# Loading q in 6 KB rows, with the layouts that follow from it, in a fused attention and token-mixing kernel

## The chip, the cores and the metric

The kernel runs on one core of one Trainium2 chip. The metric is device time in microseconds (us), the median over a kernel's executions. Each run is called fast or slow by its clock and by how far it lies above the fastest of its kernel. Matrix products are on TensorE (PE in the profile, PEld its weight loads), element-wise work on VectorE (DVE), exponentials on ScalarE (ACT), casts on GpSimd (POOL). Most DMAs are issued by SyncE (SP).

## The reference, cut to what matters

```python
# q [8, 16, 384, 64], k and v [8, 4, 384, 64]; float32
k, v   = np.repeat(k, 4, axis=1), np.repeat(v, 4, axis=1)
scores = np.matmul(q, k.transpose(0, 1, 3, 2)) / 8
attn   = softmax(scores)                       # over the keys
x      = np.matmul(attn, v).transpose(0, 2, 1, 3).reshape(8, 384, 1024)
wq, wk = x @ w_q, x @ w_k                      # [8, 384, 64]
W_tok  = np.einsum('bsd,btd->bst', wq, wk) / 8
mixed  = np.einsum('bst,btd->bsd', W_tok, x)
out    = np.maximum(mixed, 0.0) @ w_out        # [8, 384, 1024]
```

## The kernel before

A scheduler in the kernel's own code decides the order of instructions when the kernel is built, with estimates of each engine's clock. Eight batches overlap: while one batch is in attention, earlier ones are in the mixing part. These are the parts that the change and the argument touch.

```python
P, C, G, D = 128, 3, 4, 64    # partitions, groups of 128 tokens, heads per key head, head size

def ld(dst, src, a, z, c0=0, c1=C):   # token = 3 p + c: 768 B runs for each head
    nc.sync.dma_start(out=dst[:, a:z, c0:c1],
                      in_=src[b, a:z].rearrange("h (p c) d -> p h c d", p=P)[:, :, c0:c1])
...
# scores: two matmuls on the two row halves of the array
for u in range(2):
    nc.tensor.matmul(out=ps[:, u, :], lhsT=KT[lo:hi, kp * C + kc, :],
                     rhs=QT[lo:hi, t0:t0 + G, :].rearrange("k i p -> k (i p)"), ...)
...
# attend: after 12 matmuls, divide by the row sum ("the scaling"); 96 of these in the run
xnats[b] = x_p.tile([P, C, Hq, D], BF16, name="xnat", bufs=3)
nc.vector.reciprocal(out=rcp, in_=avv[:, :, D])
nc.vector.tensor_tensor(out=xnats[b][:, c, h0:h0 + G, :], in0=avv[:, :, :D],
                        in1=rcp.to_broadcast([P, G, D]), op=ALU.mult)
...
# output of 128 tokens: 512 KB, one 4 KB row for each partition
dst = out[b].rearrange("(p c) n -> c p n", c=C)[c]
nc.sync.dma_start(out=dst, in_=osb)
...
def after_s(b, s):                    # called after score group s of batch b
    n = b + 1
    if b == 0 or n >= B: return
    if s == 0:    load(n)
    elif s == 5:  cast(n); start_tr(n)
    elif s in (9, 11, 13, 15): tr_dma(n, (s - 9) // 2)
```

The softmax here doesn't subtract the row's maximum and nothing guards it: scores larger than these inputs give would overflow.

## Time and profile before

| | before |
|---|---|
| median of 3 runs (range) | 224.09 us (223.12 to 225.83) |
| profiled run: its time (slow state), its span | 226.12 us, 224.3 us |
| batch 2's first score starts | 45.45 us |
| from there to the end of the last matmul | 175.3 us |
| last output and end | 3.6 us |

The span is the sum of the last three rows, and I use these three terms.

This one profile of the kernel before is of a run that the record calls slow, and its clock shows it: 0.58 for 6.5 us from 45.5 us on, after TensorE had waited 2.9 us for q. The run `scaling_alone` below (one execution, its state unknown) begins with the same kernel. There TensorE waited 2.6 us at the same place and kept its full clock. The two lines are batch 2's first score, with the wait before it, and the stretch from 45.5 to 52 us (its columns are explained in the prediction; the 1.00 is the clock):

```profile
45.04 0.39 PE L259 MATMUL sc<-QT,KT 64*128 64x512 bf16 x2 [2.62 <-DMA QT<-qb]
...
45.50:52.00 6.50, 6.50 (x84) 3.53 (x83) 3.77 (x11) 5.38 (x6) 1.22 (x4) 1.00 1.02 267
```

In that execution the first two terms are 45.0 and 172.9. So some 2.4 us of the 175.3 above are not in every execution. Fast runs of the kernel before have a mean clock of 0.992 to 1.000, this one 0.985.

### The profile page before, as it was taken

The page shows a single profiled execution, that of the slowest core. Times are in us where ns is not written, and L with a number is a line of the kernel's source. Part 1 is how long each engine was busy: PE and PEld are TensorE (multiplying, and loading weights), DVE is VectorE, ACT ScalarE, POOL GpSimd, SP SyncE. Part 2 cuts the span into 40 slices and gives each one's busy share as a digit, 9 for nine tenths or more (in the row PEclk, how much of TensorE's full clock was granted, in tenths as well). Part 3 has the DMA queues.
Part 4 walks back from the last instruction along what each step waited for, and adds up shares of the span by engine and source line. Part 5 has one row for each costly group of instructions (what it writes and reads, how often), then busy time and mean ns, then how long its engine had stood idle before and what let it go on. Part 6 is the DMA issues. An engine that isn't in the chain of part 4 may idle for free.

```text
span 224.3 us, 5470 instructions
## 1 busy us (share of the span) xinstructions
PE 214.2 (95%) x2217; PEld 113.6 (51%) x2244; DVE 145.2 (65%) x365; ACT 140.6 (63%) x146; POOL 52.1 (23%) x97
## 2 busy tenths in 40 slices
PE   8999999589999999999999999999999999999993
PEld 5666665245545545454555546554555553434441
DVE  2355786834697758865887648874679569576332
ACT  3599998747788778887887887887888600000000
POOL 1385678406300540045016100620000000000000
PEclk9999999959999999999999999999999999999999
DMA  6996999999399979999999998989224422242424
GB/s 174 324 327 170 410 386 325 136 237 323 65 183 215 335 166 187 222 338 216 223 229 342 154 213 260 281 205 154 99 91 53 143 93 93 93 190 93 180 101 187
DMA packets 71688, 46.09 MB, mean 205 GB/s; under 512 B 42736, under 2 KB 67568, under 8 KB 71664
## 3 DMA queue, kind: packets, MB, share of 16 engines
q1 hardware_dynamic: 71520, 45.62, 77.6%
q8 instruction: 17, 0.28, 0.5%
q10 hardware_dynamic: 144, 0.13, 0.2%
q14 instruction: 7, 0.06, 0.1%
HBM read 23.59 MB, written 12.58 MB: 161 GB/s over the span
## 4 chain that ended last, share of the span: by engine, by line
PE 74%; DMA 14%; DVE 3%; SPq 3%; POOL 3%; issue 1%; DVEq 0%
PE bank L408 37%; PE bank L282 13%; PE sc L259 12%; DMA qraw<-in_q_dram 12%; PE bank L331 4%; SPq L129 3%; PE bank L384 3%; PE bank L362 2%; DMA QT<-qb 2%; PE bank L322 1%; POOL qb L158 1%; DVE osb L421 1%; PE bank L349 1%; DVE msb L389 1%; POOL wqk_sb L596 1%
## 5 line engine op out<-in xcount | busy, mean ns | idle before, releaser
L263 ACT ACTIVATE pt<-sc 128x1024 bf16<-128x1024 f32 x144 | 138.9, 1023 | 34.6 <-PE sc L259 34.4
L408 PE MATMUL bank<-wout_sb,msb 128*128 128x512 bf16 x357 | 91.7, 382 | 1.3 <-issue 0.5
L408 PEld LDWEIGHTS <-msb 128*128 128x128 bf16 x384 | 33.8, 98 | 42.4 <-issue 13.7
L259 PE MATMUL sc<-QT,KT 64*128 64x512 bf16 x288 | 47.5, 387 | 3.1 <-DMA QT<-qb 2.9
L282 PEld LDWEIGHTS <-pt 128*128 128x128 bf16 x1152 | 41.9, 98 | 15.8 <-issue 9.9
L282 PE MATMUL bank<-vext,pt 128*128 128x65 bf16 x1152 | 46.9, 195 | 0.4 <-DVE osb L421 0.2
L421 DVE COPY osb<-bank 128x512 f32<-128x512 f32 (+1 forms) x49 | 33.1, 677 | 21.7 <-PE bank L408 20.5
L289 DVE TENSOR_TENSOR xnat<-bank,rcp 128x256 bf16<-128x256 f32 x96 | 40.8, 425 | 3.3
L389 DVE TENSOR_SCALAR msb<-bank 128x384 bf16<-128x384 f32 x64 | 32.5, 551 | 9.5 <-PE bank L384 9.0
L287 DVE RECIPROCAL rcp<-bank 128x4 f32<-128x4 f32 x96 | 16.9, 176 | 17.6 <-PE bank L282 16.7
L158 POOL CAST qb<-qraw 128x768 bf16<-128x768 f32 x30 | 24.0, 827 | 17.4 <-DMA qraw<-in_q_dram 15.1
L153 POOL CAST kb<-kraw 128x192 bf16<-128x192 f32 x30 | 9.2, 347 | 67.3 <-DMA kraw<-in_k_dram 67.3
L259 PEld LDWEIGHTS <-KT 64*128 64x128 bf16 x288 | 12.4, 94 | 24.1 <-issue 17.2
L117 PE MATMUL bank<-idle 128*128 128x256 bf16 x80 | 14.8, 324 | 1.0 <-DVE idle L562 1.0
L331 PE MATMUL bank<-xT,wqk_sb 128*128 128x384 bf16 x64 | 11.7, 327 | 0.0
L117 PEld LDWEIGHTS <-idle 128*128 128x128 bf16 x80 | 7.9, 114 | 6.6 <-issue 4.0
L384 PE MATMUL bank<-wT,Csb 64*128 64x384 bf16 x32 | 10.6, 332 | 0.4 <-DVE rcp L287 0.3
L384 PE MATMUL bank<-wq,Csb 64*128 64x384 bf16 x32 | 10.6, 332 | 0.0
L599 POOL CAST wout_sb<-wld 128x1024 bf16<-128x1024 f32 x8 | 8.1, 1040 | 4.1 <-DMA wld<-in_moe_w_out_dram 4.1
L366 DVE CAST Csb<-bank 128x512 bf16<-128x512 f32 x8 | 5.5, 688 | 5.2 <-PE bank L362 5.2
L337 DVE CAST wT<-bank 128x384 bf16<-128x384 f32 x8 | 4.5, 558 | 6.7 <-PE bank L331 6.7
L323 DVE COPY xT<-bank 128x1024 bf16<-128x1024 bf16 x10 | 6.9, 688 | 2.5 <-PE bank L322 2.5
(33 smaller groups left out, 70.1 us busy)
## 6 DMA issues: line engine op xcount, KB each, us to landing
out_dram<-osb SPq DMA_DIRECT2D x23, 512.0 KB, 3.1
qraw<-in_q_dram SPq DMA_DIRECT2D x15, 768.0 KB, 7.4
wld<-in_moe_w_out_dram SPq DMA_DIRECT2D x4, 1024.0 KB, 9.5
kraw<-in_k_dram SPq DMA_DIRECT2D x7, 384.0 KB, 4.3
vraw<-in_v_dram SPq DMA_DIRECT2D x7, 384.0 KB, 8.9
qraw<-in_q_dram SPq DMA_DIRECT2D x1, 512.0 KB, 5.3
kraw<-in_k_dram SPq DMA_DIRECT2D x2, 192.0 KB, 3.7
vraw<-in_v_dram SPq DMA_DIRECT2D x2, 192.0 KB, 6.3
```

Source lines behind the costliest of these rows:

```text
L117: nc.tensor.matmul(out=bank_ps[i][:, :256], lhsT=idle[:, :P], rhs=idle, start=True, stop=True)
L158: eng.tensor_copy(out=nats[b][1][:, :, kp, :, u, :].rearrange("p c i d -> p i c d"), in_=raws[b][2][:, h0:h0 + G])
L259: nc.tensor.matmul(out=ps[:, u, :], lhsT=KT[lo:hi, kp * C + kc, :], rhs=QT[lo:hi, t0:t0 + G, :].rearrange("k i p -> k (i p)"), start=True, ...
L263: nc.scalar.activation(out=pt.rearrange("k u i p -> k u (i p)"), in_=ps, func=AF.Exp, scale=attn_scale)
L282: nc.tensor.matmul(out=ps[:, i * DE:i * DE + D + 1], lhsT=tiles[kc][:, u, i, :], rhs=vext[:, 2 * kp + u, kc, :D + 1], start=(kc == 0), sto ...
L287: nc.vector.reciprocal(out=rcp, in_=avv[:, :, D])
L289: nc.vector.tensor_tensor(out=xnats[b][:, c, h0:h0 + G, :], in0=avv[:, :, :D], in1=rcp.to_broadcast([P, G, D]), op=ALU.mult)
L331: nc.tensor.matmul(out=ps, lhsT=wqk_sb[:, dc, :], rhs=xT[:, dc].rearrange("d c p -> d (c p)"), start=(dc == 0), stop=(dc == DC - 1))
L384: nc.tensor.matmul(out=bank_ps[i][:, :S], lhsT=Csb[lo:hi, j * P:(j + 1) * P], rhs=w[lo:hi, :], start=True, stop=True)
L389: nc.vector.tensor_scalar_max(out=msb[:, dc, :], in0=bank_ps[i][:, :S], scalar1=0.0)
L408: nc.tensor.matmul(out=ps, lhsT=msbs[b][:, dc, c * P:(c + 1) * P], rhs=wout_sb[:, dc, half * NH:(half + 1) * NH], start=(nd == 0), stop=(n ...
L421: nc.vector.tensor_copy(out=osb[:, n0:n1], in_=ps[:, n0 - half * NH:n1 - half * NH])
```

## The change

Its intent is larger packets and an earlier start. A partition of q no longer holds one token triple of all heads but a stretch of 24 neighbouring tokens of one head, which lies in DRAM as one 6 KB row. Weights are loaded with eight neighbouring rows on a partition. Two things follow from this. The features of x must be stored in the order of the weight rows, so the scaling now writes to `[P, C, DC, P]`: neighbouring features of a head go to addresses 128 elements (256 bytes) apart. And a tile of transposed q holds 16 stretches by 8 tokens, so one output tile consists of 16 runs of 8 neighbouring tokens. Beside that, batch 2 is loaded and cast before attention begins, x is transposed in halves of 64 tokens, and each batch's x transposes may begin while its attention still runs.

```diff
-                              in_=src[b, a:z].rearrange("h (p c) d -> p h c d", p=P)[:, :, c0:c1])
+            src = q[b].rearrange("(u a) (s t) d -> (a s) u t d", u=2, t=C * M)   # M = 8
+            nc.sync.dma_start(out=qraw[:, :, c0 * M:c1 * M], in_=src[:, :, c0 * M:c1 * M])
 ...
-                             rhs=QT[lo:hi, t0:t0 + G, :].rearrange("k i p -> k (i p)"),
+                             rhs=QT[lo:hi, c * M:(c + 1) * M, kp * H:(kp + 1) * H].rearrange(
+                                 "k m (i s) -> k i m s", i=G),
 ...
-            xnats[b] = x_p.tile([P, C, Hq, D], BF16, name="xnat", bufs=3)
+            xnats[b] = x_p.tile([P, C, DC, P], BF16, name="xnat", bufs=3)
+            chain_open(b)
 ...
-        nc.vector.tensor_tensor(out=xnats[b][:, c, h0:h0 + G, :], in0=avv[:, :, :D],
-                                in1=rcp.to_broadcast([P, G, D]), op=ALU.mult)
+        nc.vector.tensor_tensor(
+            out=xnats[b][:, c].rearrange("p e (h r) -> p h r e", r=r)[:, h0:h0 + G],
+            in0=avv[:, :, :D].rearrange("p i (r e) -> p i r e", r=r),
+            in1=rcp.unsqueeze(2).unsqueeze(3).to_broadcast([P, G, r, DC]), op=ALU.mult)
 ...   # x_tr: full transposes become pairs of half transposes on two row groups
-        dst = out[b].rearrange("(p c) n -> c p n", c=C)[c]
+        dst = out[b].rearrange("(s c m) n -> c m s n", c=C, m=M)[c]
 ...
-    nc.sync.dma_start(out=wqkld[:, :, 0, :], in_=moe_w_q.rearrange("(c p) h -> p c h", p=P))
+    nc.sync.dma_start(out=wqkld[:, :, 0, :], in_=moe_w_q.rearrange("(p c) h -> p c h", p=P))
 ...   # w_k and w_out in the same way
+    load(2)          # before attention, behind the weights
 ...
+    cast(2)
```

## The prediction

> **What bounds the kernel now.** I first read the page's busy shares, then its 40 slices, then stretches of time, and only then the chain of waits and the order of TensorE.
>
> ```profile
> PE 214.2 (95%) x2217; PEld 113.6 (51%) x2244; DVE 145.2 (65%) x365; ACT 140.6 (63%) x146; POOL 52.1 (23%) x97
> PE   8999999589999999999999999999999999999993
> ACT  3599998747788778887887887887888600000000
> ...
> 25.00:42.40 17.40, 17.30 (x259) 10.44 (x257) 13.80 (x38) 16.45 (x18) 13.25 (x18) 1.00 1.15 325
> 42.40:45.50 3.10, 0.23 (x6) 0.08 (x2) 1.64 (x5) 1.15 (x2) 0.00 (x1) 0.78 1.04 179
> 45.50:52.00 6.50, 6.42 (x45) 2.80 (x47) 2.24 (x6) 3.14 (x4) 1.22 (x4) 0.58 1.01 257
> 75.00:178.00 103.00, 101.23 (x1149) 53.24 (x1166) 73.18 (x193) 82.77 (x86) 20.05 (x36) 1.00 0.87 206
> ```
>
> The columns of the last four lines are the stretch in us, busy us of PE, weight loads, DVE, ACT and POOL, granted clock, DMA share and GB/s. TensorE is full except for one hole at 42.4 to 45.5, after which its clock is 0.58 for 6.5 us. In batches 0 and 1 ScalarE is full as well (digits of 9) and TensorE's time is partly filler, 80 matmuls on an idle tile. From 52 us on TensorE alone is the bound. The chain of waits names the hole's cause:
>
> ```profile
> 24.88 14.96 DMA qraw<-in_q_dram
> 39.90 1.60 POOL qb L158 x2
> 41.53 3.79 DMA QT<-qb
> 45.45 0.61 PE sc L259 x2
> ```
>
> Columns are start and length in us. The second half of batch 2's q was issued at 24.88, queued behind the output weights, landed at 39.9, was cast on GpSimd and transposed by DMA; batch 2's first score could not start before 45.45.
>
> "Busy" hides TensorE's pace, so I take start-to-start times, from the timeline of TensorE:
>
> ```profile
> 51.44 0.61 PE L259 MATMUL sc<-QT,KT 64*128 64x512 bf16 x4
> 51.98 0.93 PE L282 MATMUL bank<-vext,pt 128*128 128x65 bf16 x24
> 52.74 0.61 PE L322 MATMUL bank<-ident,xnat 128*128 128x128 bf16 x8
> 53.18 0.81 PE L408 MATMUL bank<-wout_sb,msb 128*128 128x512 bf16 x3
> 53.93 0.61 PE L259 MATMUL sc<-QT,KT 64*128 64x512 bf16 x4
> ```
>
> Four score matmuls (two pairs on the two row halves of the array) take 0.54 us, attention 0.76/24 = 0.032, a full transpose 0.44/8 = 0.056, an output matmul 0.216 (three plus a change take 0.75). Each change between full-array, row-tiled and column-tiled matmuls adds 0.095: score to full is 0.31 where full to full is 0.216. The rest of the trace gives 0.162 for a wqk matmul, 0.163 for a pair of relu-mix matmuls, 0.216 for a pair of mix matmuls.
>
> I counted matmuls and changes in the built order of the program from batch 2's first score on: 108 score pairs x 0.220 = 23.8, 888 attention 28.4, 384 output 82.9, 56 wqk 9.1, 29 relu-mix pairs 4.7, 21 mix pairs 4.5, 77 transposes 4.3, 5 fillers 0.5, 140 changes 13.3: 171.5 us. Measured: from 45.45 to the end of the last matmul at 220.74, 175.3. Of the 3.8 extra, 2.5 lie before 52 us (slow clock: 6.5 us for 4.0 us of work) and 1.2 in the 169 us after. So the tail of the run is priced within 1%, and the end is set by when batch 2 starts, plus this sum, plus 3.6 us of last copy, output DMA and finish (220.74 to 224.3).
>
> **What the Trainium skill says.** "DMA: Bandwidth & Descriptors", section "Why small descriptors are slow (HBM only)": each packet has a fixed overhead. The trace agrees: packets of 256 B take 18 ns, 768 B 38, 4 KB 161 (medians), so 14, 20 and 25 bytes per ns on an engine; over two microseconds of 768 B loads the queue moves some 327 GB/s, in the 4 KB loads 400 to 417. "TensorE: Matmul & The Clock Gate", Part 1: an idle window of about 3.4 us halves the clock. The trace agrees in kind: 3 us idle, then 0.58. The same page, Part 3, "The mechanism": row-tiled matmuls start about 4 ns apart and run together; the score pairs and their weight loads do so here (4 ns). "Advanced Engine Details and Errata", section "SBUF Cachelines": 16-byte lines, at least two hits on a line for full speed. No run here shows this; it matters for two new access patterns below.
>
> **The change part by part.**
>
> 1. Loads. q comes as two 6 KB rows per partition (2 KB pieces for batch 0) instead of 768 B (256 B for the first piece); w_q and w_k in 2 KB rows instead of 256 B, w_out in 8 KB. k and v stay at 768 B. Estimated from the rates above (327 for k and v, 380 for 2 KB, 410 for more), in order of issue: batch 0 6.6 us, batch 1 6.2, wqk 1.4, w_out 10.1, starting at 1.8 us, so w_out ends at 26.1 where GpSimd waited for it until 34.1 before.
>
> 2. Load and cast of batch 2 are issued before attention begins, behind the weights: k by 27.3, q by 31.1, landing near 32.8 (before, 39.9). Six casts of about 0.53 us, then a DMA transpose (3.7 us from issue to landing): K near 35, the first third of Q near 38. The hole goes if batch 2's first score isn't due earlier than that.
>
> 3. When it is due. ScalarE takes 0.945 us per exponential when fed (24 in 22.67 us), and the 36 of batches 0 and 1 free the slot for batch 2's first score at 7.5 + 35 x 0.945 = 40.6 if it never starves; before it idled 1.06 us at 10.4 and 0.9 at 34. The first score hardly moves: it needs 512 KB of q instead of 256 KB, cast in 512-element halves, but in larger packets (7.1 before; I take 7.0). One third of q now serves both key pairs, so six score groups follow at once. TensorE's own work between the two first scores is 33.3 us by the same prices (34.6 before), of which 48 fillers; that gives 40.3. I take 41.1 with half a microsecond of starving. Against 45.45 this is 4.3 us, and the 2.5 us of slow clock go with the hole: 6.8 together.
>
> 4. TensorE from there: four output matmuls have moved ahead of batch 2 (-0.9), for batch 0's relu starts them from its first product. x is transposed in halves of 64 tokens on two row groups: 72 pairs x 0.032 (the pace of a 65-column matmul) = 2.3 instead of 56 x 0.056 = 3.1 (-0.8), even though all of batch 1 is done so instead of by DMA. wk: 21 x 0.030 instead of 0.056 (-0.5). Three fillers fewer (-0.3), two changes more (+0.2). Sum 169.2, against 171.5: -2.3.
>
> 5. x transposes inside attention open each chain as early as its x is there, not after the batch's attention. From batch 2 on TensorE is full anyway, so this only reorders work; in batches 0 and 1, where ScalarE sets the pace, it replaces filler. Its gain is already in part 4.
>
> 6. VectorE: 24 half copies of 0.42 for x instead of 10 of 0.69, and 18 instead of 12 for q and k: some 4 us over the run, beside TensorE's work, at 0.71 of its time in the steady stretch.
>
> Sum: 41.1 + 169.2 + 1.2 (the bubbles of before) + 3.6 = 215.1 us of span. The median before, 224.09, is nearly its profiled span, so I predict 215.1, 4.0% faster.
>
> **Rivals.**
>
> A. The new access patterns cost more than they save. Scores read q in runs of 16 elements (32 bytes, two whole lines, so by the page's rule free); if the stream slowed by a tenth, 108 pairs x 0.022 = 2.4 us follow. The scaling on VectorE (0.425 us, 96 times) writes single bf16 elements 256 bytes apart; if it doubled, 72 x 0.425 = 31 us would fall on an engine with 29% of 126 us free. It wouldn't become the bound by its sum, but banks would come free late; 218 to 221. Against it: the scaling is already slow per element (256 in 0.425 us, where a bf16 copy does 512 in 0.42), so scattered writes may hide; nothing in the trace excludes it.
>
> B. The half transposes don't run together. Two weight loads per pair, if serial at 0.032 each, make 72 x 0.032 = 2.3 us more: 217.4. The score pairs, whose weight loads start 4 ns apart, speak against it. A transpose now also needs two of the four banks.
>
> C. The hole is only moved: batch 2's Q arrives late after all, or batch 3's transposes meet the output writes. The margin is 41.1 - 38 = 3 us. If GpSimd is late by 5 us, 2 us of hole and its clock return: 219.
>
> D. TensorE isn't the bound but ScalarE: 108 exponentials of batches 2 to 7 x 0.945 = 102 us, until 143 us. It stays far from the end, so a faster start is not swallowed there.
>
> **Range and chances.** Below 215 there is little: at most 1 us from the start and 1 us of bubbles, so 213. Above, A, B and C each have a chance of a fifth or less and cost 2 to 5 us: 219. Two per cent faster is 219.6. Faster 0.89, within 2% 0.09, slower 0.02.
>
> **What would show it.** Batch 2's first score at 40 to 42 us, no empty slice at 42 to 45, granted clock 1.00 there; a q landing before 34 us; start-to-start 0.54 for two score pairs, 0.26 for eight half pairs; the scaling at 0.43 us on VectorE; 170.4 us from that score to the last matmul. A scaling of 0.6 us or more, score pairs above 0.23, half pairs at 0.06, or a wait for Q in batch 2 or 3 would make me wrong, by the amounts above.

## More of the kernel before

The following lines are two rows of the page's costliest groups: line, engine, operation, tiles, shape and count, then busy time in us and mean ns of one, then idle time just before them and its releaser.

```profile
L289 DVE TENSOR_TENSOR xnat<-bank,rcp 128x256 bf16<-128x256 f32 x96 | 40.8, 425 | 3.3
...
L287 DVE RECIPROCAL rcp<-bank 128x4 f32<-128x4 f32 x96 | 16.9, 176 | 17.6 <-PE bank L282 16.7
```

The first is the scaling: 96 instructions of 256 elements per partition, 425 ns each, 40.8 us of VectorE's 145.2.

## The result, and the profile after

| | before | after |
|---|---|---|
| median (range), 4 fast runs each | 223.61 us (222.86 to 225.83) | 269.0 us (268.14 to 270.5) |
| ratio of fast runs, 95% interval | | 1.2017 (1.1913 to 1.2122) |
| profiled span | 224.3 (slow run) | 266.4 |
| batch 2's first score | 45.45 | 54.24 |
| from there to the end of the last matmul | 175.3 | 203.0 |
| tail | 3.6 | 9.1 |

A ratio here is the mean time of one kernel's fast runs over that of the other's of the same rounds (the profiled ones seem to be left out), so it is not quite the ratio of the medians that I quote.

The change made the kernel 20% slower, where I predicted 4% faster. The page of the changed kernel, its busy shares, two of its 40 slices and its chain of waits by engine and by line:

```profile
PE 218.6 (82%) x2374; PEld 110.0 (41%) x2405; DVE 218.6 (82%) x384; ACT 142.3 (53%) x146; POOL 53.3 (20%) x110
...
PE   5967877779987988888978889879988978999960
...
DVE  2399988999989888999899889998999989775430
...
DVE 55%; PE 35%; issue 5%; DMA 2%; ACT 0%; SPq 0%; DVEq 0%
DVE xnat L311 36%; PE bank L429 18%; DVE msb L410 6%; DVE osb L442 5%; PE bank L303 4%; PE sc L278 4%; DVE rcp L308 3%; PE bank L129 2%; PE bank L351 2%; DMA qraw<-in_q_dram 2%; PE bank L383 2%; PE bank L235 1%; PE bank L405 1%; DVE xT L241 1%; DVE Csb L387 1%
```

Before, TensorE's row was all nines but for the hole. Now it is sevens and eights through the steady stretch, and VectorE's row holds the nines. The chain of waits, of which TensorE's share was 74% before, runs through VectorE for 55%, and through one line, L311, for 36%. That line is the scaling. Its row among the costliest groups, with that of the reciprocal just ahead of it:

```profile
L311 DVE TENSOR_TENSOR xnat<-bank,rcp 128x256 bf16<-128x256 f32 x96 | 124.6, 1298 | 4.3
...
L308 DVE RECIPROCAL rcp<-bank 128x4 f32<-128x4 f32 x96 | 25.9, 270 | 4.6 <-PE bank L303 3.9
```

The same 256 elements take 1298 ns instead of 425: 96 x 0.873 = 84 us more on VectorE. The reciprocal's growth is bookkeeping. The timeline shows a reciprocal that follows a scaling starting some 0.4 us before the scaling's end and waiting for it, with that wait in its duration.

The same stretches of time that the prediction shows of the kernel before, in the changed one (columns as there: stretch, busy us of PE, weight loads, DVE, ACT, POOL, clock, DMA share, GB/s):

```profile
25.00:42.40 17.40, 13.77 (x220) 8.20 (x216) 15.81 (x29) 13.98 (x15) 10.52 (x18) 1.00 0.98 266
42.40:45.50 3.10, 1.94 (x32) 1.15 (x32) 2.02 (x5) 1.30 (x2) 0.28 (x1) 1.00 0.92 295
45.50:52.00 6.50, 5.11 (x63) 2.48 (x62) 6.35 (x11) 5.33 (x7) 3.81 (x10) 1.00 0.61 229
75.00:178.00 103.00, 86.16 (x946) 42.52 (x962) 93.38 (x161) 64.57 (x67) 21.36 (x47) 1.00 0.97 197
```

VectorE is busy for 15.81 of 17.4 us already in the first stretch, and for 93.4 of 103 us in the last, where it had 73.2 before. Batch 2's hole is gone, as intended (the clock of 45.5 to 52 is 1.00 instead of 0.58), but that is worth nothing while VectorE is behind. (From 54.2 to 60 us the clock is 0.70 here too, after two waits for VectorE of 1.1 and 0.8 us.) How VectorE sets the pace is seen in the chain of waits in order of time (start, length in us, what):

```profile
98.72 0.19 DVE rcp L308
...
98.94 1.30 DVE xnat L311
...
100.30 1.30 DVE xnat L311
101.59 0.52 DVE osb L442
```

Two scalings stand back to back, and the copy of an output bank to SBUF can begin only after both.

A second change is at the end. The timeline of the last DMA issues, before and then after:

```profile
219.77 1.79 SPq L423 DMA_DIRECT2D out_dram<-osb  x2
...
221.57 0.37 ACTq L423 DMA_DIRECT2D out_dram<-osb  x1
```

```profile
256.26 3.93 SPq L444 DMA_DIRECT2D out_dram<-osb  x2
...
258.06 1.20 ACTq L444 DMA_DIRECT2D out_dram<-osb  x1
```

The last piece is issued 2.7 us before the end of the span in the kernel before (221.57 of 224.3) and 8.3 us in the changed one (258.06 of 266.4), for the same 128 KB. I had not thought of this pattern at all.

### The profile page after: what moved, and what is told of

It is laid out like the page before. It is cut to its first block, busy times and chain, and to the rows that moved or that the text cites. A ratio compares the mean times of both kernels' runs of the same rounds, so it can differ in the third digit from the quotient of the medians.

```text
span 266.4 us, 5820 instructions
## 1 busy us (share of the span) xinstructions
PE 218.6 (82%) x2374; PEld 110.0 (41%) x2405; DVE 218.6 (82%) x384; ACT 142.3 (53%) x146; POOL 53.3 (20%) x110
## 4 chain that ended last, share of the span: by engine, by line
DVE 55%; PE 35%; issue 5%; DMA 2%; ACT 0%; SPq 0%; DVEq 0%
DVE xnat L311 36%; PE bank L429 18%; DVE msb L410 6%; DVE osb L442 5%; PE bank L303 4%; PE sc L278 4%; DVE rcp L308 3%; PE bank L129 2%; PE bank L351 2%; DMA qraw<-in_q_dram 2%; PE bank L383 2%; PE bank L235 1%; PE bank L405 1%; DVE xT L241 1%; DVE Csb L387 1%
## 5 line engine op out<-in xcount | busy, mean ns | idle before, releaser
L283 ACT ACTIVATE pt<-sc 128x1024 bf16<-128x1024 f32 x144 | 140.4, 1021 | 70.7 <-PE sc L278 70.5
L311 DVE TENSOR_TENSOR xnat<-bank,rcp 128x256 bf16<-128x256 f32 x96 | 124.6, 1298 | 4.3
L429 PEld LDWEIGHTS <-msb 128*128 128x128 bf16 x384 | 32.8, 97 | 53.1 <-issue 24.9
L442 DVE COPY osb<-bank 128x512 f32<-128x512 f32 (+1 forms) x49 | 35.3, 722 | 11.2 <-PE bank L429 11.1
L410 DVE TENSOR_SCALAR msb<-bank 128x384 bf16<-128x384 f32 x64 | 35.5, 595 | 2.8 <-PE bank L405 2.6
L181 POOL CAST qb<-qraw 128x512 bf16<-128x512 f32 x45 | 25.9, 619 | 19.3 <-issue 10.9
L308 DVE RECIPROCAL rcp<-bank 128x4 f32<-128x4 f32 x96 | 25.9, 270 | 4.6 <-PE bank L303 3.9
L129 PE MATMUL bank<-idle 128*128 128x256 bf16 x69 | 13.1, 325 | 4.0 <-DVE rcp L308 2.4
L241 DVE COPY xT<-bank 128x512 bf16<-128x512 bf16 x24 | 9.8, 451 | 2.4 <-PE bank L235 2.3
L235 PE MATMUL bank<-ident,xnat 64*128 64x64 bf16 x192 | 5.5, 190 | 6.8 <-DVE xnat L311 5.5
L383 PE MATMUL bank<-xnat,wkN 128*64 128x512 bf16 x48 | 6.7, 387 | 2.5 <-DVE wkN L372 2.5
```

The source lines that it names most:

```text
L129: nc.tensor.matmul(out=bank_ps[i][:, :256], lhsT=idle[:, :P], rhs=idle, start=True, stop=True)
L181: copy(out=nats[b][1][:, c * M:(c + 1) * M, u, :], in_=raws[b][2][:, u, c * M:(c + 1) * M])
L283: nc.scalar.activation(out=pt.rearrange("k u i p -> k u (i p)"), in_=ps, func=AF.Exp, scale=attn_scale)
L311: nc.vector.tensor_tensor(out=xnats[b][:, c].rearrange("p e (h r) -> p h r e", r=r)[:, h0:h0 + G], in0=avv[:, :, :D].rearrange("p i (r e) ...
L410: nc.vector.tensor_scalar_max(out=msb[:, dc, :], in0=bank_ps[i][:, :S], scalar1=0.0)
L429: nc.tensor.matmul(out=ps, lhsT=msbs[b][:, dc, c * P:(c + 1) * P], rhs=wout_sb[:, dc, half * NH:(half + 1) * NH], start=(nd == 0), stop=(n ...
```

## The experiments

The theory after reading the traces: the scattered write of the scaling is what makes VectorE the bound (nearly all of the loss), and the new output pattern adds the tail, and perhaps more where VectorE doesn't hide it. The rivals: the scaling is slow because of its 4-dimensional operands and the double broadcast, not because of where it writes; TensorE's score stream with runs of 16 elements is what slows; the x transposes inside attention are what load VectorE.

"Rows wrong" means that a kernel computes the right numbers but writes some of them to other rows of the output. The reference's neighbouring rows differ by only 1.3%, so the comparison of outputs on the chip cannot see this. I therefore also ran seven kernels in a simulator with q 25 times and k 10 times as large, where neighbouring rows differ by 1.16 of their norm. The kernels before and after, `x_nat`, `x_nat_perm_warm` and `before_plus` agreed with the reference to 0.009; `x_nat_rows` and `before_8x16` were off by 1.15, as intended. (`before_scatter`, `before_hoist` and `x_nat_perm` agree to 0.009 as well; `after_rows` is off by 1.15.)

### x_nat: the changed kernel with x stored as before

```diff
-            xnats[b] = x_p.tile([P, C, DC, P], BF16, name="xnat", bufs=3)
+            xnats[b] = x_p.tile([P, C, Hq, D], BF16, name="xnat", bufs=3)
 ...
+        nc.vector.tensor_tensor(out=xnats[b][:, c, h0:h0 + G, :], in0=avv[:, :, :D],
+                                in1=rcp.to_broadcast([P, G, D]), op=ALU.mult)
 ...   # and w_q, w_k, w_out loaded as "(c p)" again
```

> The changed kernel with x written in its natural order again (256 neighbouring elements per scaling, w rows as in the kernel before), all else as changed. Theory (the scattered write makes the scaling 1.3 us and VectorE the bound): scaling back to 0.43 us, about 221 us, that is my predicted 215 plus some 5.6 us of a slow output write at the end that the changed trace shows. Rival (the half transposes with two banks, or the new order, clog VectorE): scaling faster but the time stays above 240.

Measured: 236.94 us median of four, 235.71 of the three fast runs, ratio to before 1.0588 (1.048 to 1.0696). The profiled run was a slow one (238.63), so I use its trace for what waits, not for small differences. The scaling is 425 ns again, and VectorE's busy share is 62%. So undoing the scattered write takes back some 33 us of the 45 lost, and the theory on the scaling holds. But the time is 15 us above the 221 that I expected, and some 13 us over the kernel before remain, of which the tail explains less than half: the terms of its span are 44.7, 182.9 and 9.2. There was a second cost in the middle. In the group of instructions on transposed q, these lines are the DMA transposes (duration of the issue in ns, minimum, median, maximum) and what TensorE's scores waited for (us, times):

```profile
L218 SPq DMA_TRANSPOSE QT<-qb x18: 1243/1992/3978, 36.3 to 162.6; - x18
...
  DMA QT<-qb: 9.0, 4
```

Four times TensorE waited for late q, 9.0 us in all.

### before_scatter: the kernel before with x stored as in the changed one

```diff
+            xnats[b] = x_p.tile([P, C, DC, P], BF16, name="xnat", bufs=3)
 ...   # the changed kernel's tensor_tensor, and its "(p c)" weight loads
```

> The kernel before with only the scattered x (and the w rows that go with it). Theory: scaling near 1.3 us, VectorE busy rises by 96 x 0.87 = 84 us to some 229 us, time 255 to 270 us. Rival: the scaling is slow only together with the changed order, so below 235 us here.

Measured: 267.21 us, ratio 1.197 (1.1889 to 1.205), terms 53.7, 208.4 and 3.6, within what I expected. This one part, put into the kernel before, costs as much as the whole change. It contains no half transposes, no new q and no new output, so the rivals on the score stream and on the x transposes fall.

### scaling_alone: the scaling in variants, by itself

Appended to the kernel before, each variant three times, 256 elements per partition, on data without meaning. The numbers of interest are durations of single instructions.

> The kernel before, and after its end on idle engines the scaling with different destinations, three times each. Theory (cost per element that goes to a place far from the last one): contiguous 0.43 us with three or four dimensions; a step of 4 or 8 bytes still near it, steps of 16 to 256 bytes near 1.3 us; plain copies scattered the same slow too. Rival (the four-dimensional pattern or its broadcast is what costs): 1.3 us for the four-dimensional pattern with contiguous destination.

Some rows of the groups, whose lines stand for these variants: L652 the changed kernel's write, L648 a plain 3-dimensional one with a step of 16 bytes between elements, L647 with 8 bytes, L646 with 4 bytes, L645 the changed kernel's 4-dimensional operands with a contiguous destination, and L659 a copy of the same data on ScalarE to the changed kernel's addresses.

```profile
L659 ACT CAST wld<-bank 128x256 bf16<-128x256 f32 x3 | 3.9, 1296 | 91.7 <-DVE wld L658 91.7
...
L652 DVE TENSOR_TENSOR wld<-bank,rcp 128x256 bf16<-128x256 f32 x3 | 3.9, 1294 | 0.1
L648 DVE TENSOR_TENSOR wld<-bank,rcp 128x256 bf16<-128x256 f32 x3 | 3.9, 1289 | 0.1
...
L647 DVE TENSOR_TENSOR wld<-bank,rcp 128x256 bf16<-128x256 f32 x3 | 2.2, 725 | 0.1
L646 DVE TENSOR_TENSOR wld<-bank,rcp 128x256 bf16<-128x256 f32 x3 | 1.3, 443 | 0.1
...
L645 DVE TENSOR_TENSOR wld<-bank,rcp 128x256 bf16<-128x256 f32 x3 | 1.3, 424 | 0.1
```

The rival on dimensions and broadcast falls: the same 4-dimensional instruction with a contiguous destination takes 424 ns (L645), and a 3-dimensional one with a step takes 1289 ns (L648). What counts is the distance between written elements. Two bf16 elements in 16 bytes cost 725 (I had expected this step of 8 bytes to stay near 430), one 1289, and larger steps cost no more (32 bytes 1226, 64 bytes 1268, the changed kernel's 256 bytes 1294, 2 KB 1295). That is (1294 - 424) / 256 = 3.4 ns for each element. A copy on ScalarE pays about the same (1296, against 372 contiguous) and so does one on GpSimd, from SBUF (1318 against 397), so I see nothing to gain from moving the scaling to another engine. One variant on VectorE I cannot explain: a plain copy from SBUF instead of PSUM to the same scattered addresses took 737 ns, a product from SBUF 1295.

### x_nat_out: x_nat with the last batch's output cut into DMAs of 16 rows

```diff
+                for m in range(M):        # one DMA for each of the 8 outermost steps
+                    nc.sync.dma_start(out=dst[m], in_=osb[m * 16:(m + 1) * 16, :])
```

> x in natural order and the last batch's output written as eight DMAs of 16 rows instead of one of 8 x 16 rows. Theory (a destination with 8 outermost steps is spread over 8 of the 16 DMA engines): end of the last matmul to end of span back from about 9 us to 4 to 5 us, so 215 to 217 us. Rival (the tail is long for another reason, as address order): same as x_nat.

Measured: 243.98 us, with three of its four executions, the profiled one among them, slow; the one fast run took 239.06, against 234.82 to 238.17 for the fast runs of `x_nat`. So it is no better, and there is no ratio worth giving. My remedy for the tail was wrong, and its expectation of 215 to 217 us failed. In the trace the tail is even longer, 15.4 us against 9.2, though each of these DMAs has 16 outermost steps. That counts against the theory as far as this run goes; it changed the number of DMAs as well, and its trace is of a slow run, so I read no more out of it. The three runs that follow test the theory in another way.

### x_nat_rows: x_nat with the output pattern of before (rows wrong)

```diff
-        dst = out[b].rearrange("(s c m) n -> c m s n", c=C, m=M)[c]
+        dst = out[b].rearrange("(p c) n -> c p n", c=C)[c]
```

> x in natural order, and the output written with the row pattern of the kernel before (128 outermost steps). Rows land in the wrong places on purpose: only the time is of interest. Theory (a destination of 8 outermost steps halves the write rate, which makes the tail long and makes the DMA transposes of q late): waits for QT from 9 us to under 1 us, tail from about 8 us to 3.6 us, so 214 to 218 us, my predicted figure. Rival (QT is late because the loads are packed closer, or the transposes are issued earlier): the tail shortens but the QT waits stay, so 228 to 233 us.

Measured: 220.28 us, ratio 0.9833 (0.9749 to 0.9918), terms 44.7, 170.6 and 3.5. I expected 214 to 218; the waits went as the theory said, the time missed by 2.3 us (the start, and a span that I had taken for a time: see the part on the prediction). With both patterns undone, what is left of the change is a gain of 1.7%, not clear of 2%, and TensorE is the bound again. Its chain of waits by engine, and the transposes of q:

```profile
PE 87%; ACT 5%; DMA 2%; issue 2%; DVE 1%; SPq 0%; DVEq 0%
...
L218 SPq DMA_TRANSPOSE QT<-qb x18: 1232/1413/2083, 37.0 to 148.1; - x18
```

No wait for a DMA transpose of q is left in that group. So the output pattern cost `x_nat` some 15 us (fast runs, 235.71 - 220.28). The slow trace of `x_nat` shows where: 5.7 us more in the tail (9.2 - 3.5), and in the middle the 9.0 us of waits for q; the clock was at half rate after two of these, 3.4 us each.

### before_8x16: the kernel before with the new output pattern alone (rows wrong)

```diff
-        dst = out[b].rearrange("(p c) n -> c p n", c=C)[c]
+        dst = out[b].rearrange("(s c m) n -> c m s n", c=C, m=8)[c]
```

> The kernel before with only the output pattern of 8 x 16 rows (rows in wrong places on purpose). Theory: writes at about 150 GB/s, tail longer by 4 to 6 us, and some waits for QT or xT added: 229 to 240 us. Rival: under 226 us.

Measured: 248.73 us, ratio 1.1155 (1.1092 to 1.1218), terms 44.7, 193.8 and 8.9. The output pattern alone costs 26 us, more than the 6 to 17 that I expected. It waits for q as `x_nat` did, only longer (us in all, times, the longest):

```profile
PE sc L259 <- DMA QT<-qb: 16.8, 4, 6.4
```

Why is seen in the DMA share in tenths over the last 29 us before the tail, in 40 slices, first in the kernel before (190 to 219 us), then here (208 to 237 us). Only output is moved then.

```profile
DMA  0000393008900197000004930592007900098002
```

```profile
DMA  4410154545735456354201455455454554445554
```

Before, each output tile is a short burst at nearly the full share of the 16 DMA engines. Here the share stays near one half and there is hardly a gap. From the packets of the traces: a 512 KB tile is 128 packets of 4 KB in all three patterns. Before, they take 1.44 us from the first's start to the last's end, 163 ns each on average with 14.5 in flight. With the new pattern, 640 packets in a row took 19.85 us in the changed kernel, 3.97 us per tile, 226 ns each on average with 7.3 in flight: half as many, each 1.39 times as long. (The median is 159 ns, as before; one packet in ten takes over 414.) And TensorE finishes an output tile in 16 x 0.216 = 3.46 us when it does nothing else, so near the end the writes fall behind, which is the tail. In the middle, loads and transposes share the queue with them.

The new destination has 8 outermost steps, where the old one had 128. The Trainium skill states this case on the page "DMA: Bandwidth & Descriptors", section "Rules for kernel authors": an outermost dimension smaller than 16 confines a DMA to at most that many engines. The 7.3 packets in flight agree. I had read another section of this very page for the prediction, and not this one.

### x_nat_perm: x_nat with 16 outermost steps, true rows

The products `w` that decide the order of output tokens are permuted in the copy that is made of them anyway, so that the output goes to 16 stretches of 8 neighbouring rows.

```diff
-        nc.vector.tensor_copy(out=wT, in_=ps)
+        nc.vector.tensor_copy(out=wT[Dh:2 * Dh, :], in_=ps[Dh:2 * Dh, :])
+        perm = ps[:Dh, :].rearrange("h (c m s) -> h c s m", c=C, m=M)
+        for w in (wT[:Dh, :], wq2[Dh:2 * Dh, :]):
+            nc.vector.tensor_copy(out=w.rearrange("h (c s m) -> h c s m", c=C, m=M), in_=perm)
 ...
-        dst = out[b].rearrange("(s c m) n -> c m s n", c=C, m=M)[c]
+        dst = out[b].rearrange("(s c m) n -> c s m n", c=C, m=M)[c]
```

> A correct version: x natural, and the tokens put back in order where wq is copied out of PSUM (three copies a batch instead of two), so that the output goes out as 16 x 8 rows. Theory (as many engines write as there are outermost steps, up to 16): 215 to 219 us, faster than before by 2 to 4%. Rival (any pattern but the plain one writes slowly): as x_nat, 235 us and more.

Measured: 221.32 us, ratio 0.9927 (0.9866 to 0.9988), terms 44.7, 170.5 and 4.2. I had expected 215 to 219. From 235.71 (fast runs) to 221.32 us by exchanging two dimensions of a destination, with the copies that this needs. The rival, that any pattern but the plain one writes slowly, falls, for this one isn't the plain one either. A tile now takes 2.15 us with 14.6 packets in flight, of 245 ns each: about as many at once as before, but the packets are still slower on average than the 163 ns with 128 outermost steps, and why is open. It no longer holds anything up but 0.7 us of the tail.

### before_hoist: the kernel before with batch 2 loaded and cast before attention

```diff
+    load(2)            # behind the weights
 ...
+    cast(2)            # behind their casts; after_s leaves batch 2 out
```

> The kernel before with only batch 2's load and cast moved ahead of attention, and its transposes issued earlier. Theory (the hole at 42 us is a matter of order alone): hole and slow clock go, 5 us less, 217 to 219 us. Rival (q in 768-byte rows arrives too late all the same): 221 us or more.

Measured: 221.86 us, ratio 0.9963 (0.9897 to 1.0029), terms 43.7, 172.9 and 3.6. So my 217 to 219 failed, and the gain of the early load alone is not resolved. Against the full-clock execution of the kernel before (45.0 and 172.9) batch 2 starts 1.3 us earlier and the rest takes as long: that execution had no slow clock to save. In its trace TensorE still waits 1.9 us for a DMA transpose of q, once. I take it that batch 2's load, which stands behind all of w_out, and its casts are still late; `before_plus` therefore puts them between the halves of w_out.

### after_rows: the changed kernel with only the output pattern undone (rows wrong)

```diff
-        dst = out[b].rearrange("(s c m) n -> c m s n", c=C, m=M)[c]
+        dst = out[b].rearrange("(p c) n -> c p n", c=C)[c]
```

> The changed kernel with only the output row pattern of the kernel before (rows in wrong places on purpose), the scattered scaling kept. Theory (VectorE is the bound there, so late transposes don't add; only the long tail does): 5 to 6 us less than the changed kernel, 262 to 265 us. Rival (the two faults add): 25 us less, 244 us.

Measured: 264.13 us, ratio 1.1855 (1.1784 to 1.1926), terms 55.5, 202.9 and 3.5, as expected. The output pattern costs the changed kernel the 5.6 us of its tail (9.1 - 3.5) and nothing in the middle: 203.0 with it and 202.9 without. There VectorE is so far behind that slow DMAs are hidden. That settles how the two costs combine. On top of `x_nat_rows` (220.3 us) the scattered write costs 44 us (`after_rows`), the output pattern some 15 (`x_nat`, fast runs), and both 49 (the changed kernel).

### x_nat_perm_warm and before_plus: two versions that may beat both

`x_nat_perm_warm` adds 14 filler matmuls on an idle tile while TensorE waits for the first q:

```diff
     tr_k(0, 0, 1)
+    keep_busy(1700)
```

`before_plus` keeps the kernel before with its loads of q, its x and its output, and takes the other parts of the change: batch 2's load and cast early (between the halves of w_out), half transposes of x, transposes of batch 1's x on TensorE and x transposes inside attention.

```diff
-            chain_open(b)                  # after the batch's attention
+            chain_open(b)                  # at its first product
 ...
+        if dc == 4:
+            load(2)
```

> The correct version x_nat_perm with 14 filler matmuls where TensorE waits for the first q. Theory (its idle 2 us before the first q cools the clock, and that delays the first scores): first exponential 0.5 to 1 us earlier, batch 2's first score at 43 us instead of 44.6, 219.5 to 220.5 us. Rival (the landing of q sets it): no difference to x_nat_perm, 221.3 us.

> The kernel before with its q layout, x layout and output pattern kept, and the rest of the change: batch 2 loaded ahead (between the halves of w_out), half transposes of x, x transposes and chains inside attention. By the prices of the prediction: batch 2's first score at 42 to 43, then 169.2 + 1.2 + 3.6 us: 216 to 218 us, faster by 2 to 3%. Rival (q rows of 768 bytes land too late): a wait for QT in batch 2 remains, 219 to 221.

Measured: `x_nat_perm_warm` 219.24 us, ratio 0.9839 (0.9795 to 0.9882), terms 42.8, 170.5 and 4.2; `before_plus` 219.15 us, ratio 0.9861 (0.9796 to 0.9926), terms 42.7, 171.1 and 3.5. The first is a little below its range, the second above its 216 to 218, in the rival's, though TensorE waits only once for a DMA transpose of q, 0.4 us. Both beat both kernels, the one before by 1.4 to 1.6%, though neither is clear of 2%. `before_plus` has none of the new layouts. So what the change could gain came from its other parts, and the 6 KB rows of q, which forced the new output order, added nothing that these runs resolve.

Why the filler gains is seen in the timeline of the start, first of `x_nat_rows`, which has the changed kernel's start, then of `x_nat_perm_warm` (start, length, engine, instruction, idle time before and its releaser):

```profile
6.70 0.61 PE L235 MATMUL bank<-ident,qb 64*128 64x64 bf16 x16 [2.23 <-ACT qb L181]
...
8.42 1.04 PE L278 MATMUL sc<-QT,KT 64*128 64x512 bf16 x4
```

```profile
6.66 0.41 PE L235 MATMUL bank<-ident,qb 64*128 64x64 bf16 x16 [0.54 <-ACT qb L181]
...
7.65 0.61 PE L278 MATMUL sc<-QT,KT 64*128 64x512 bf16 x4
```

After 2.23 us of idle time TensorE does the same work at a lower pace, 1.04 us for four score matmuls instead of 0.61. Bridged, the first score is due 0.8 us earlier, and 1.2 us earlier than in `x_nat_perm` (8.82, after 2.62 us of idle time). The profiled run of the changed kernel itself escaped it: 1.73 us idle, then 0.60 us, with its first score at 7.18. In `after_rows`, whose start is the same code, 1.99 us idle was followed by 1.04 us and a first score at 8.19. So the start is on an edge. The length of the idle time alone doesn't decide: 2.62 us of it slowed `x_nat_perm` here, and 2.62 us before batch 2's first score left the clock of `scaling_alone` at 1.00.

## Why the prediction was wrong, point by point

The record said 215.1 us, the result was 269.0. The prediction's three terms were 41.1, 170.4 and 3.6 us of span; they came out at 54.2, 203.0 and 9.1. The difference of 51.2 us is nearly all of the 53.9 us missed. The rest is a slip in the comparison. 215.1 is a span, and the time would be 1.8 us more, 216.9. I took the span for a time because the median before, 224.09, lay near the span of 224.3; but that profile is of a slow run that took 226.12 us. The ranges for `x_nat_rows` and `before_plus` have the same slip.

The slow profile also led me to count a gain that not every run has to give: the 2.5 us of slow clock after the hole. They are in the profiled run, and not in the full-clock execution of the same kernel (`scaling_alone`: 172.9 instead of 175.3). The span of such a run would be some 45.0 + 172.9 + 3.6 = 221.5 us by my estimate, so that a span of 215.1 would have been 2.9% faster and not 4.0%.

**The step that failed is part 6, VectorE's work.** It added 4 us for copies and kept the scaling at 0.425 us, so that VectorE stayed at 0.71 of its time beside TensorE. Measured, the scaling takes 1.298 us, and VectorE is the bound. Rival A had named the danger and underpriced it: "if it doubled, 72 x 0.425 = 31 us would fall on an engine with 29% of 126 us free", with "218 to 221" and the argument that "scattered writes may hide". The mechanism, a write to a new 16-byte line for each element, was right. The size was 3.05 times instead of 1 or 2: 72 x 0.873 = 63 us. Priced so, the prediction's own sum shows the new bound. In the 134.6 us from batch 2's first score to 180 us, VectorE of the kernel before is busy for 93.7; with 63 more it is 157, more than there is. In the changed kernel VectorE is busy for 153.4 of the 166.8 us of that part (54.24 to 221). "It wouldn't become the bound by its sum" was right for a doubling and false for the measured size; `x_nat` and `before_scatter` show it from both sides. The argument that the scaling "is already slow per element" is no argument: the slow pace of 425 ns did not hide the cost of the new lines. The rule that the prediction quotes, two hits on a line for full speed, spoke against a write with one hit per line; I used it only to call the scores free.

**A second step was missing.** The tail was put down at 3.6 us as before, and no rival had the output's pattern in it, though the diff shows the new destination. It is a write at half the packets in flight for each output, and `before_8x16`, `x_nat_rows` and `after_rows` show its cost. In the changed kernel it costs 5.6 us; with TensorE as the bound it costs 15 (`x_nat`) to 26 (`before_8x16`).

**Step 1, loads: half right.** The packets of q and w_out grew as said. The fourth piece of w_out was in SBUF for GpSimd at 30.2 us, where I estimated 26.1. One reason is that w_q and w_k gained nothing: the trace shows their packets at 256 B still, at 209 GB/s between 16 and 18 us. The destination is written in runs of 64 float32, which are 256 B.

**Step 2, batch 2 early: right in kind.** Its first q cast began at 35.3 us instead of near 32.8 and the DMA transposes of q at 36.5, in time. The hole and its slow clock are gone (the windows above).

**Step 3, the due time: mis-sized by 3.6 us.** In `x_nat_rows`, free of the two failures, batch 2's first score starts at 44.7 instead of 41.1. The first exponential there starts at 9.07, not 7.5, through the slow start shown above, and up to batch 2 ScalarE is 2.3 us behind its pace, not 0.5: 9.07 + 35 x 0.945 + 2.3 = 44.4. With the start bridged (`x_nat_perm_warm`) it is 42.8. I had taken the first score as hardly moving, without asking what TensorE does while it waits for a larger first piece of q.

**Step 4, TensorE's remaining work: right.** 170.4 us predicted, 170.6 in `x_nat_rows` and 170.5 in `x_nat_perm`. Runs of 16 elements cost the score stream nothing: start-to-start times of two pairs stay at 0.54. The half transposes of x ran at 29 to 31 ns a pair in `x_nat_rows` against the 32 assumed, so rival B was wrong. The method of counting the built order with prices from the trace is sound for the engine it was applied to. It was applied to one engine only.

**Step 5** is consistent with that sum: x transposes inside attention changed the order and not the total. **Step 6**, 4 us more on VectorE, is 146.5 us busy in `x_nat_rows` against 145.2, so rather less. **Rival C** didn't occur in the changed kernel, whose transposes of q were in time; its thought, transposes that meet output writes, came true in `x_nat`. **Rival D** didn't occur.

**The chances.** I gave "slower" (by over 2%) 0.02 while stating that "nothing in the trace excludes" the cost of the scattered write. A single instruction that runs 96 times, with a pattern never measured, on an engine at 71%, deserved a tail of its own in the range, not 5 us.

What stays open: why 4 KB packets take 245 ns with 16 outermost steps and 163 with 128, why a scattered copy from SBUF costs only 737 ns, and which of `before_plus`'s parts carries its gain, for it was measured as one.

## What to carry to other kernels

When a layout change is made for one consumer (here larger weight packets), look at the innermost step of every write that must now produce it, and price it by elements: a bf16 element on its own 16-byte line cost 3.4 ns more on VectorE here and 3.6 on ScalarE and GpSimd (one variant, a plain VectorE copy from SBUF, cost less). Put the largest dimension outermost in a DMA's destination: 8 outermost steps made a write of 512 KB 2.8 times as long as 128 did. And before trusting a sum over the bounding engine, make the same sum for the next one with its new pattern at two or three times the old duration.

## What the Trainium skill lacked or had wrong

- "Advanced Engine Details and Errata", section "SBUF Cachelines", has no cost, and its "at least two hits" was not enough here: two bf16 elements on each 16-byte line took 725 ns for 256 elements, four took 443, eight 424, and one 1226 to 1295. That ScalarE (1296 ns) and GpSimd (1318 ns) pay as VectorE does for such writes is not said there either.
- "DMA: Bandwidth & Descriptors" has the rule that explains the slow output ("Rules for kernel authors"). It lacks that packets were also slower in the two patterns with few outermost steps on the destination: on average 163 ns for 4 KB with 128 steps, 245 with 16, and 226 with 8, the last with half the packets in flight. Three patterns were measured, and the cause is open.
- "TensorEngine Tiling (Array Packing)", section "Key Properties", says that a change of tiling mode drains TensorE, without a number. The trace before has 0.095 us for each change, and with this price the sum over the changed order agreed with `x_nat_rows` to 0.2 us.
- No page that I read gives the pace of transposes in pairs on two row halves: 29 to 31 ns for a pair of half transposes of x in `x_nat_rows`.
